# Value sums in four 32-row tiles instead of two 64-row tiles, in a recurrent attention kernel on TensorE

## The chip, the cores and the metric

The kernel runs on one core of one Trainium2 chip. The metric is the device time of one execution in microseconds (us), as the median of several. The engines that matter are TensorE (PE, matmuls; its weight loads are listed as PEld), VectorE (DVE), ScalarE (ACT), GpSimd (POOL) and the DMA queues, of which SyncE (SP) issues most. [...]

## The reference

Two blocks are computed twice, one after the other, on x of 2048 rows by 512. Block A is attention with a recurrent memory: the rows are taken in 64 segments of 32, and each segment sees 8 memory rows ahead of its own 32.

```
for s in range(64):
    h = concat(mem, layernorm(x)[32*s : 32*s + 32])        # 40 rows x 512
    q, k, v = h Wq, h Wk, h Wv                             # 32 heads of 128
    p = softmax(mask(q k^T * scale))                       # 40 x 40 for each head
    o = (p v) Wo                                           # 40 x 512
    mem = o[0:8]                                           # goes into the next segment
    out[s] = o[8:40]
x = x + out
```

The memory rows see everything; of the others, a row sees the memory and the rows up to itself. Block B is a gated MLP with a product over the rows (a 2048 x 2048 matrix). The segments of block A depend on each other through `mem`, so that a segment's projections can't start before the output projection of the one before.

## The kernel before

**Rows of a segment.** Each segment has 8 memory rows and 32 others. The projections of a segment run on 32 rows: the 8 memory rows and the first 24 of the others. The last 8 of each segment's rows are projected ahead, for the four segments of a block of 128 rows together (`b_units`, `b_even`, `b_light`, from line 809), and their output projection follows later (`y_part`). These are the *fill* matmuls: `fill()` issues the next few of them at set places of the segment, a step being mostly 4, 8 or 16 matmuls. Their results (KX, VX and the last columns of QQ) make the "own" part below.

**Heads.** The 32 heads are two halves r of 16. In a half, head 4i + g has index i = 0..3 and group g = 0..3. Group g lies in partitions 32g to 32g + 31: in S and E the partition is 32g + key row.

**One segment** (`segment`, from line 1055) is written out by hand. The order of instructions on PE, DVE and ACT is the order of the code (a manual schedule), so that each engine takes its instructions in this order, and waits between engines are semaphores:

- Projections of q and k, `qk(0)`, `qk(2)`, `qk(1)`, `qk(3)` (L753): ACT copies each to `rows` (L1072), DVE transposes it into QQ or KA (L1075).
- `scores(r)`: 16 matmuls of 40 columns (L1098) and 4 of 64 (L1102) into psS, in column tiles of 32. `exps(r)` (L1107, ACT) writes S.
- `close(r)` (L1110, DVE) multiplies S by a mask and writes E. E is held twice: E[:, r, s] for s = 0, 1 holds the groups with g % 2 = s and zeros for the others, so that one matmul over 64 partitions (two groups) gives both groups' results in columns of their own.
- `v_mm(r)` (L753): the value projections, into psK for half 0 (copied to VA by DVE, L1196) and psV for half 1 (copied to VA by ACT, L1211).
- `sums_zero` (L1121): the softmax sums of half 0's memory rows, 16 matmuls of 64 columns. `inverse` (ACT, L1164 Ln and L1165 Exp) makes 1/sum, Rm.
- `pv(r)`: value sums, 8 matmuls of 80 columns with VA as weights (L1147) and 2 of 128 with VX (L1150), in 64-row tiles into psO[r], two banks for each half.
- `sums_tokens` (L1139) gives the sums of all other rows into psT, `sums_one` (L1130) those of half 1's memory rows into psO[1].
- `memory_out(r)` (L1168, DVE): value sums of the memory rows times Rm, into uT. `spare1` issues spare work between the two.
- The output projection of the memory rows: `wo_pairs` for half 0 (L930, into px) and `wo_rest` for half 1 (L937, into psO[1]'s spare columns); `fold_side`, `fold` and `build_hA` (L1034 to L1047) add the parts and transpose them into hT, where the next segment's projections read them. Fill matmuls stand between.
- Off that path: ACT makes Rt, the inverse of psT (L1245, L1248); DVE writes the token outputs, `tok_out` (L1171) and `last_out` (L1174).

**PSUM** in block A: accA and accB (one bank each, for fills, psm, psV, px), `att` (two banks: psQ, then psS, then psT) and `attO[0]`, `attO[1]` (two banks each; psK uses `attO[0]`, psO[0] and psO[1] both).

The order around the change, of half 1's values and the sums:

```
v_mm(1, psW, (0, 1)); scores(1); exps(1); v_mm(1, psW, (2,)); sums_zero(pN); v_mm(1, psW, (3,))
invert = inverse(0, pN); copy VA[:, 1] (ACT); invert(); close(1)
fill(); pv(0); sums_tokens(psT); sums_one(); pv(1); memory_out(0); spare1(E); fill()
inverse(1, psO[1][:, :, 320:384])(); memory_out(1); wo_pairs(px, uT_cur); wo_rest(pw, uT_cur)
```

Of the kernel before, what the change touches and what calls it, by code (L numbers as in the profile page):

```python
# [14 lines left out]
P = 128  # L15
# [51 lines left out]
def _consts(ctx, tc, c, b_sp, between):  # L67
# [11 lines left out]
    own = maskf[:, 160:224].rearrange("p (i q) -> p i q", i=4)  # L79
# [4 lines left out]
    for q in range(0, P, 32):  # L84
        blk = maskf[q:q + 32, 0:160].rearrange("p (i q) -> p i q", i=4)[:, :, 8:32]
        nc.gpsimd.affine_select(out=blk, in_=blk, compare_op=ALU.is_ge, fill=0.0, base=8,
                                pattern=[[0, 4], [1, 24]], channel_multiplier=-1)
        last = own[q:q + 32, :, 8:16]
        nc.gpsimd.affine_select(out=last, in_=last, compare_op=ALU.is_ge, fill=0.0, base=0,
                                pattern=[[1, 4], [4, 8]], channel_multiplier=-1)  # L90
    maskN = cp.tile([P, 2, 224], BF16, name="maskN")
    nc.vector.memset(maskN[:], 0.0)
    for gs in range(4):
        nc.vector.tensor_copy(maskN[32 * gs:32 * gs + 32, gs % 2, :], maskf[32 * gs:32 * gs + 32, :])
    ones = cp.tile([P, P], BF16, name="ones")
    nc.vector.memset(ones[:], 1.0)
    half = cp.tile([P, 2, 32], BF16, name="half")
    nc.vector.memset(half[:], 0.0)
    for g in range(2):
        nc.vector.memset(half[64 * g:64 * g + 64, g, :], 1.0)  # L100
# [9 lines left out]
    c.update(maskN=maskN, ones=ones, half=half)  # L110
# [596 lines left out]
def a_block(tc, c, rows, front, MV_in, RS_in, MV_out, RS_out, ahead, wo, S, first):  # L707
# [4 lines left out]
    maskN, ones, half = c["maskN"], c["ones"], c["half"]  # L712

    with ExitStack() as ctx:
# [19 lines left out]
        ps_pool = ctx.enter_context(tc.tile_pool(name="a_ps", bufs=1, space=PSUM))  # L734
        ps1_pool = ctx.enter_context(tc.tile_pool(name="a_ps1", bufs=1, space=PSUM))

        accA = _Tagged(acc_pool, "accA", 1)
        accB = _Tagged(acc_pool, "accB", 1)
        att = _Tagged(ps_pool, "att", 1)
        attO = [_Tagged((ps_pool, ps1_pool)[r], f"attO{r}", 1) for r in range(2)]  # L740
# [126 lines left out]
        def early_turn():  # L867

            for k, G in enumerate(EARLY):
                pT = (att, attO[1])[k].tile([P, 2 * DM * 2], BF16, name="pT")  # L870
# [16 lines left out]
        def early_units():  # L887

            for n, (j, G, k) in enumerate((j, G, k) for j, G in ((0, 2), (0, 3), (2, 2)) for k in range(2)):
                ps = (attO[0], attO[1], att)[n % 3].tile([P, 2, 512], F32, name="psP")  # L890
# [164 lines left out]
        def segment(s, fill, spare1, spare2, spare3, tail, loads):  # L1055
# [11 lines left out]
            E = segp.tile([P, 2, 2, 224], BF16, name="E", bufs=1)  # L1067
# [16 lines left out]
            def own(q):  # L1084

                return q.rearrange("p (i b e) -> p i b e", i=4, b=2)
# [4 lines left out]
            def scores(r):  # L1091
# [3 lines left out]
                for i in range(4):  # L1095
                    for g in range(4):
                        n = 4 * i + g
                        mms.append(nc.tensor.matmul(pS[32 * g:32 * g + 32, 40 * i:40 * i + 40], lhsT=KA[:, r, n // 2, :, n % 2], rhs=QQ[:, r, n // 2, :, n % 2],  # L1098
                                                    start=(i == 0), stop=True, tile_position=(0, 32 * g), skip_group_check=True))
                for g in range(4):  # L1100
                    q = QQ[:, r].rearrange("p (i g) q two -> p i g two q", i=4)[:, :, g // 2, g % 2, :]
                    mms.append(nc.tensor.matmul(own(pS[32 * g:32 * g + 32, 160:224]), lhsT=KX[r][:, g, :], rhs=ends(q),  # L1102
# [9 lines left out]
            def e_all(e, lo, hi):  # L1112

                return e[:, :, 0:160].rearrange("p n (i q) -> p n i q", q=40)[:, :, :, lo:hi]

            def e_own(e, b):
                return e[:, :, 160:224].rearrange("p n (i b e) -> p n i b e", i=4, b=2)[:, :, :, b, :]

            def sums_zero(pN):

                return [nc.tensor.matmul(pN[32 * cg:32 * cg + 32, 64 * g:64 * g + 64], lhsT=half[:, g, :], rhs=e_own(E[:, 0], 0) if k else e_all(E[:, 0], 0, 8),  # L1121
                                         start=False, stop=True, tile_position=(0, 32 * cg), skip_group_check=True)
                        for k in range(2) for g in range(2) for cg in range(4)]

            def sums_one():

                for k in range(2):
                    for g in range(2):
                        e = E[64 * g:64 * g + 64, 1]
# [340 lines left out]
```

## Time and profile before

| | |
|---|---|
| median of 3 runs | 1608.67 us (1607.46 to 1610.44) |
| the profiled execution | 1610.67 us, its span 1609.0 us |
| granted TensorE clock | 1.0 |
| instructions | 90845 |
| segments of block A in the span | 128 (64 in each of two passes) |

A row of the timeline gives start and duration in us, engine, line, operation, output<-inputs, the tile (rows*columns of the array, for PE), the shape and a count: instructions of one kind that follow each other closely are one row, with the start of the first and the time that their union covers. The bracket says how long the engine was idle before it and what released it. A row of a group has instead: count, busy us in all, mean ns of one, idle us before them. Matmuls overlap: a matmul's row lasts from the first column going in until the last result, so a row's duration is longer than the step to the next row.

### The profile page before, as it was taken

The numbers are of one execution on the slowest core, as the hardware profiler recorded it, in microseconds if no ns is written. First come the engines' busy times: TensorE is split into PE (matmuls) and PEld (weight loads), VectorE is DVE, ScalarE is ACT, GpSimd is POOL, SyncE is SP. The second block draws the span as 40 slices with busy tenths as digits, with TensorE's granted clock in tenths as the row PEclk, the third lists the DMA queues.
The fourth block names the chain that finished last, engine by engine and source line by source line (L and its number), as shares of the span: only waits on it lengthen the run. The fifth ranks groups of instructions, "written<-read, shape, count | busy, mean of one in ns | idle before, by whom it ended". The sixth has DMA issues, their size and how long they took to land.

```text
span 1609.0 us, 90845 instructions
## 1 busy us (share of the span) xinstructions
PE 1577.9 (98%) x40998; PEld 979.7 (61%) x40998; DVE 1068.8 (66%) x3064; ACT 1052.1 (65%) x2279; POOL 307.5 (19%) x674
## 2 busy tenths in 40 slices
PE   6899999999999999999999999999999999999999
PEld 3566666666666666566656666666666666665565
DVE  3667666667777776784456666666677667768622
ACT  4677777777777777670057777777777777776400
POOL 6211111112211222320011111111222112224000
PEclk9999999999999999999999999999999999999999
DMA  9411221213211332378951112111232123425697
GB/s 360 137 57 43 43 44 45 48 40 76 83 50 40 87 87 61 102 176 176 208 160 45 46 48 46 50 44 50 73 89 72 47 72 95 97 56 174 146 186 169
DMA packets 256861, 149.93 MB, mean 93 GB/s; under 512 B 189592, under 2 KB 232192, under 8 KB 256472
## 3 DMA queue, kind: packets, MB, share of 16 engines
q1 hardware_dynamic: 242552, 97.94, 27.3%
q0 software_dynamic: 13920, 46.18, 8.5%
q8 instruction: 321, 5.26, 1.3%
q14 instruction: 68, 0.56, 0.1%
HBM read 60.21 MB, written 39.55 MB: 62 GB/s over the span
## 4 chain that ended last, share of the span: by engine, by line
PE 56%; DMA 1%; DVE 1%; issue 0%; ACT 0%; SPq 0%; POOL 0%; DVEq 0%; POOLq 0%
PE pg L401 9%; PE psQ L753 7%; PE psK L753 7%; PE psb L753 5%; PE pz L300 4%; PE psO L937 4%; PE px L930 3%; PE psV L753 3%; PE psm L753 3%; PE py L444 3%; PE pwB L949 2%; PE psO L1147 2%; PE psT L1139 1%; PE psS L1098 1%; PE pw L1422 0%; PE psS L1121 0%
## 5 line engine op out<-in xcount | busy, mean ns | idle before, releaser
L753 PEld LDWEIGHTS <-hT 128*32 128x32 bf16 x12288 | 343.5, 96 | 261.4 <-DVE hT L1047 18.3
L753 PE MATMUL psV<-Wv_sb,hT 128*32 128x512 bf16 x2048 | 166.0, 379 | 0.0
L1072 ACT CAST rows<-psQ 128x512 bf16<-128x512 f32 x256 | 144.8, 589 | 24.2 <-PE psQ L753 21.3
L1107 ACT ACTIVATE S<-psS 128x224 bf16<-128x224 f32 x256 | 92.2, 360 | 99.7 <-PE psS L1102 99.5
L1168 DVE TENSOR_TENSOR uT<-psO,Rm 128x128 bf16<-128x128 f32 x256 | 74.7, 292 | 124.2 <-ACT Rm L1165 123.9
L1075 DVE STREAM_TRANSPOSE QQ<-rows 128x256 f32<-128x256 f32 x256 | 112.5, 440 | 66.7 <-ACT rows L1072 63.7
L1075 DVE STREAM_TRANSPOSE KA<-rows 128x256 f32<-128x256 f32 x256 | 113.0, 441 | 63.5 <-ACT rows L1072 60.7
L401 PE MATMUL pg<-z,wspT 128*128 128x344 bf16 x1024 | 154.3, 309 | 0.0
L753 PE MATMUL psK<-Wv_sb,hT 128*32 128x512 bf16 x2048 | 152.2, 378 | 0.0
L1171 DVE TENSOR_TENSOR uT<-psO,Rt 128x384 bf16<-128x384 f32 x256 | 139.9, 547 | 16.7 <-ACT Rt L1248 15.1
L1248 ACT ACTIVATE Rt<-Rt 128x512 f32<-128x512 f32 x256 | 147.3, 622 | 4.1
L937 PE MATMUL psO<-Wo_high,uT 128*32 128x128 bf16 x8192 | 140.6, 219 | 2.4 <-issue 1.6
L753 PE MATMUL psQ<-Wq_sb,hT 128*32 128x512 bf16 x2048 | 135.9, 379 | 2.7 <-DVE hT L219 1.5
L753 PE MATMUL psQ<-Wk_sb,hT 128*32 128x512 bf16 x2048 | 135.2, 379 | 0.0
L753 PE MATMUL psm<-Wq_sb,hT 128*32 128x512 bf16 x2048 | 135.2, 379 | 0.0
L753 PE MATMUL psK<-Wk_sb,hT 128*32 128x512 bf16 x2048 | 135.1, 379 | 0.0
L930 PE MATMUL px<-Wo,uT 128*32 128x256 bf16 x3840 | 133.8, 273 | 0.5 <-issue 0.4
L1245 ACT ACTIVATE Rt<-psT 128x1024 f32<-128x1024 f32 x128 | 131.2, 1025 | 3.1
L401 PEld LDWEIGHTS <-wspT 128*128 128x128 bf16 x1024 | 100.1, 98 | 53.4 <-issue 0.4
L937 PEld LDWEIGHTS <-uT 128*32 128x32 bf16 x8192 | 123.0, 97 | 12.7 <-issue 3.6
L930 PEld LDWEIGHTS <-uT 128*32 128x32 bf16 x4096 | 104.0, 97 | 24.1 <-DVE uT L1168 1.2
L1029 POOL COPY KX<-old 128x128 bf16<-128x128 bf16 x128 | 65.7, 540 | 257.3 <-PE psS L1102 148.9
(221 smaller groups left out, 2886.0 us busy)
## 6 DMA issues: line engine op xcount, KB each, us to landing
o_d<-o_sb SPq DMA_DIRECT2D x126, 64.0 KB
vb_d<-front SPq DMA_DIRECT2D x31, 256.0 KB
VX<-vb_d SPq DMA_DIRECT2D x124, 64.0 KB
ln_x<-xd SPq DMA_DIRECT2D x26, 256.0 KB
y_o<-o_d POOLq DMA_DIRECT2D x22, 256.0 KB, 3.3
xd<-y_o POOLq DMA_DIRECT2D x22, 256.0 KB, 2.8
Wq_sb<-in_A_Wq_dram POOLq DMA_DIRECT2D x8, 512.0 KB, 7.3
Wk_sb<-in_A_Wk_dram POOLq DMA_DIRECT2D x8, 512.0 KB, 9.6
```

The lines of the kernel that those rows point to most:

```text
L401: nc.tensor.matmul(pg[t][:, k, 0:344], lhsT=wsp[t][:, st, :], rhs=z(st, 344 * k, 344 * k + 344), start=(st == 0), stop=(st == NT - 1))
L753: return [nc.tensor.matmul(ps[32 * cg:32 * cg + 32, :], lhsT=lhs(kt, cg), rhs=rhs(kt, cg), start=(kt == 0), stop=(kt == KT - 1), tile_posi ...
L930: nc.tensor.matmul(px[at:at + 32, 0:256], lhsT=lhs[:, h, :], rhs=wo_rhs(h, slice(k + 2, None, -2) if h % 2 else slice(k, None, 2)), start= ...
L937: nc.tensor.matmul(pw[32 * cg:32 * cg + 32, :], lhsT=lhs[:, h, :], rhs=wo_rhs(h, cg), start=False, stop=(h == H - 1), tile_position=(0, 32 ...
L1029: eng.tensor_copy(KX[r][:].rearrange("p g (k i) -> p i g k", i=4), bs["KTB"][:, r].rearrange("p (i g) k -> p i g k", i=4)[:, :, :, 8 * j4: ...
L1072: return r, mms, copy(r[:].rearrange("p (n el two) -> p n el two", n=8, two=2), ps.rearrange("p (n two el) -> p n el two", n=8, two=2))
L1075: nc.vector.transpose(out=(QQ[:, j % 2, :, 0:32] if j < 2 else KA[:, j % 2]).bitcast(F32).rearrange("p n q one -> p n (q one)"), in_=r[:]. ...
L1107: return nc.scalar.activation(out=S[:, r], in_=psS[:, r, 0:224], func=ACT.Exp, scale=scale)
L1168: nc.vector.tensor_tensor(out=hview(uT_cur[:], r, 24, 32), in0=oview(r, 0, 8), in1=Rm[:, r].rearrange("p g (n q) -> p g n q", q=8), op=ALU ...
L1171: nc.vector.tensor_tensor(out=hview(uT_nxt[:], r, 0, 24), in0=oview(r, 8, 32), in1=rview(r, 0, 24), op=ALU.mult)
L1245: nc.scalar.activation(out=Rt[:], in_=psT[:], func=ACT.Ln)
L1248: nc.scalar.activation(out=rt, in_=rt, func=ACT.Exp, scale=-1.0)
```

## The change

- E is held once, [P, 2, 224]: for each i, 40 columns (`0:40`) and 16 columns of the own part (`40:56`). The mask has the same layout, and `scores` writes psS in it.
- `pv(r)` works in tiles of 32 rows: each group g has a matmul of its own (16 of 40 columns and 4 of 64) into a PSUM bank of its own; both halves share these four banks (columns 160r and up). `sums_one` does the same with 8 matmuls of 32 columns.
- `sums_zero` takes 8 matmuls of 32 columns and stands directly behind `scores(1)`. `divide` (DVE, a reciprocal and a product) divides half 0's memory columns of E ahead of `pv(0)`, so that `memory_out(0)` is a copy. `inverse` is gone; Rm is made for half 1 alone.
- VA's half 0 is copied by ACT and no longer by DVE.
- `sums_tokens` stands behind `pv(1)` and has 8 matmuls (256 and 64 columns) in 64-row tiles, with weights `pick` that are one for one of the two groups.
- `attO` is one tile of four banks; psK uses its first two. Three pools `pre` take the place of `att` and `attO` for the work ahead of the first segment, and are closed before it.

```
-                nc.vector.tensor_tensor(out=E[:, r], in0=S[:, r].unsqueeze(1).to_broadcast([P, 2, 224]), in1=maskN[:], op=ALU.mult)
+                nc.vector.tensor_tensor(out=E[:, r], in0=S[:, r], in1=mask[:], op=ALU.mult)
...
+                return [nc.tensor.matmul(pN[32 * g:32 * g + 32, :], lhsT=group[:, g, :], rhs=E4[:, 0, :, 40 * k:40 * k + 8],
+                                         start=False, stop=True, tile_position=(0, 32 * g), skip_group_check=True)
+                        for k in range(2) for g in range(4)]
+            def divide(pN):
+                rc = segp.tile([P, 32], F32, name="rc", bufs=1)
+                read = nc.vector.reciprocal(out=rc[:], in_=pN)
+                e = E[:, 0].rearrange("p (i c e) -> p i c e", i=4, e=8)[:, :, 0:6:5, :]
+                nc.vector.tensor_tensor(out=e, in0=e, in1=rc[:].rearrange("p (i e) -> p i e", i=4).unsqueeze(2).to_broadcast([P, 4, 2, 8]), op=ALU.mult)
+                return read
+            def tile32(out, g, lhsT, rhs, start):
+                return nc.tensor.matmul(out, lhsT=lhsT, rhs=rhs, start=start, stop=True, tile_position=(32 * g, 0), skip_group_check=True)
...
+                    for n in range(2):
+                        for g in range(2):
+                            e = E4[64 * g:64 * g + 64].rearrange("p r i c -> p (r i) c")
+                            o = psT[:, g, 256 * n:256 * n + 256].rearrange("p (n q) -> p n q", q=32)
+                            nc.tensor.matmul(o[:, :, 24:32] if k else o, lhsT=pick[64 * g:64 * g + 64, n, :], rhs=e[:, :, 48:56] if k else e[:, :, 8:40],
+                                             start=(k == 0 and n == 0), stop=True, skip_group_check=True)
...
                 for i in range(4):
-                    for g in range(2):
-                        o = psO[r][:, g, 0:320].rearrange("p (s i q) -> p s i q", s=2, i=4)[:, :, i, :]
-                        nc.tensor.matmul(o, lhsT=VA[64 * g:64 * g + 64, r, i, :], rhs=E[64 * g:64 * g + 64, r, :, 40 * i:40 * i + 40],
-                                         start=(r == 0 and i == 0), stop=True, skip_group_check=True)
+                    for g in range(4):
+                        at = 160 * r + 40 * i
+                        tile32(psO[:, g, at:at + 40], g, of(VA, g)[:, r, i, :], of(E4, g)[:, r, i, 0:40], r == 0 and i == 0)
...
+                if r == 0:
+                    nc.vector.tensor_copy(hview(uT_cur[:], 0, 24, 32), oview(0, 0, 8))
...
-            nc.vector.tensor_copy(VA[:, 0].rearrange("p i e -> p (i e)"), psK[:, 1, :])
+            nc.scalar.copy(VA[:, 0].rearrange("p i e -> p (i e)"), psK[:, 1, :])
...
-            v_mm(1, psW, (2,))
-            pN = psS[:, 0, 224:352]
+            pN = psS[:, 0, 224:256]
             other_bank(sums_zero(pN), expd)
-            v_mm(1, psW, (3,))
-            Rm = segp.tile([P, 2, 2, 64], F32, name="Rm", bufs=1)
-            invert = inverse(0, pN.rearrange("p (g q) -> p g q", g=2))
+            other_bank([divide(pN)], expd)
+            v_mm(1, psW, (2, 3))
             nc.scalar.copy(VA[:, 1].rearrange("p i e -> p (i e)"), psW[:])
-            invert()
             close(1)
-            psO = [attO[r].tile([P, 2, 512], F32, name="psO") for r in range(2)]
+            psO = attO.tile([P, 4, 512], F32, name="psO")
...
             pv(0)
             psT = att.tile([P, 2, 512], F32, name="psT")
-            sums_tokens(psT)
             sums_one()
             pv(1)
+            sums_tokens()
             memory_out(0)
...
-            inverse(1, psO[1][:, :, 320:384])()
+            Rm = segp.tile([P, 4, 32], F32, name="Rm", bufs=1)
+            nc.scalar.activation(out=Rm[:], in_=psO[:, :, 320:352], func=ACT.Ln)
+            nc.scalar.activation(out=Rm[:], in_=Rm[:], func=ACT.Exp, scale=-1.0)
             memory_out(1)
```

More of the change, by code (lines that the diff above doesn't have):

```diff
@@ L109, in _consts @@
     tctx.close()
-    c.update(maskN=maskN, ones=ones, half=half)
+    c.update(mask=mask, ones=ones, group=group, pick=pick)
     return c
@@ L711, in a_block @@
     scale = float(DH) ** -0.5
-    maskN, ones, half = c["maskN"], c["ones"], c["half"]
+    mask, ones, group, pick = c["mask"], c["ones"], c["group"], c["pick"]
     with ExitStack() as ctx:
@@ L1125, in sums_one, with of @@
+            def tile32(out, g, lhsT, rhs, start):
+                return nc.tensor.matmul(out, lhsT=lhsT, rhs=rhs, start=start, stop=True, tile_position=(32 * g, 0), skip_group_check=True)
+            def of(t, g):
+                return t[32 * g:32 * g + 32]
             def sums_one():
                 for k in range(2):
[L1128 to L1131 removed]
```

96 lines of the change are left out of this document (43 added, 53 removed).

## Prediction, on record before the changed kernel ran

> **What bounds the kernel now.** I read the page first, then the timeline of one recurrent segment out of the middle (400 to 410 us), then the groups by form for means over all segments. From the page:
>
> ```profile
> PE 1577.9 (98%) x40998; PEld 979.7 (61%) x40998; DVE 1068.8 (66%) x3064; ACT 1052.1 (65%) x2279; POOL 307.5 (19%) x674
> PEclk9999999999999999999999999999999999999999
> ```
>
> TensorE is 98% busy at full clock. A busy share does not show short gaps, because a matmul's row runs on after its columns have gone in; so I go by the starts in the timeline (start, duration, engine, line, out<-in, count).
>
> ```profile
> 400.44 1.05 PE L753 MATMUL psQ<-Wq_sb,hT 128*32 128x512 bf16 x16
> ...
> 401.93 0.28 DVE L1174 TENSOR_TENSOR front<-psO,Rt 128x128 bf16<-128x128 f32 x1
> ...
> 403.04 1.05 PE L753 MATMUL psK<-Wk_sb,hT 128*32 128x512 bf16 x16
> ...
> 404.13 0.28 PE L1098 MATMUL psS<-QQ,KA 128*32 128x40 bf16 x16
> ...
> 404.24 0.20 PE L1102 MATMUL psS<-QQ,KX 128*32 128x64 bf16 x4
> ...
> 404.27 0.82 PE L753 MATMUL psK<-Wv_sb,hT 128*32 128x512 bf16 x12
> ...
> 405.39 0.68 DVE L1196 CAST VA<-psK 128x512 bf16<-128x512 f32 x1
> ...
> 405.45 0.20 PE L1102 MATMUL psS<-QQ,KX 128*32 128x64 bf16 x4
> ...
> 405.48 0.39 PE L753 MATMUL psV<-Wv_sb,hT 128*32 128x512 bf16 x4
> ...
> 405.70 0.29 PE L1121 MATMUL psS<-E,half 128*32 128x64 bf16 x16
> 405.74 0.36 ACT L1107 ACTIVATE S<-psS 128x224 bf16<-128x224 f32 x1 [0.76 <-PE psS L1102]
> ...
> 405.81 0.39 PE L753 MATMUL psV<-Wv_sb,hT 128*32 128x512 bf16 x4
> ...
> 406.03 0.39 PE L949 MATMUL pwB<-Wo,old 128*32 128x512 bf16 x4
> ...
> 406.25 0.59 ACT L1211 CAST VA<-psV 128x512 bf16<-128x512 f32 x1
> ...
> 406.35 0.32 PE L1147 MATMUL psO<-E,VA 64*128 64x80 bf16 x8
> ...
> 406.50 0.22 PE L1150 MATMUL psO<-E,VX 64*128 64x128 bf16 x2
> ...
> 406.58 0.45 PE L1139 MATMUL psT<-E,ones 64*128 64x512 bf16 x4
> ...
> 406.86 0.22 PE L1130 MATMUL psO<-E,ones 64*128 64x64 bf16 x4
> ...
> 406.92 0.31 PE L1147 MATMUL psO<-E,VA 64*128 64x80 bf16 x8
> ...
> 407.06 0.22 PE L1150 MATMUL psO<-E,VX 64*128 64x128 bf16 x2
> 407.08 0.29 DVE L1168 TENSOR_TENSOR uT<-psO,Rm 128x128 bf16<-128x128 f32 x1 [0.56 <-ACT Rm L1165]
> ...
> 407.21 0.40 PE L949 MATMUL pwB<-Wo,old 128*32 128x512 bf16 x4
> ...
> 407.32 0.28 ACT L1164 ACTIVATE Rm<-psO 128x128 f32<-128x128 f32 x1 [0.28 <-PE psO L1150]
> ...
> 407.44 1.04 PE L930 MATMUL px<-Wo,uT 128*32 128x256 bf16 x30
> 407.63 0.31 ACT L1165 ACTIVATE Rm<-Rm 128x128 f32<-128x128 f32 x1
> 407.98 0.29 DVE L1168 TENSOR_TENSOR uT<-psO,Rm 128x128 bf16<-128x128 f32 x1 [0.27 <-ACT Rm L1165]
> 408.21 0.28 PE L930 MATMUL px<-Wo_high,uT 128*32 128x256 bf16 x2
> ...
> 408.32 1.08 PE L937 MATMUL psO<-Wo_high,uT 128*32 128x128 bf16 x64
> ...
> 410.15 1.05 PE L753 MATMUL psQ<-Wq_sb,hT 128*32 128x512 bf16 x16
> ```
>
> Four facts are to be seen. (1) Next to nothing on PE waits: each row starts when the columns of the row before are in (four matmuls of 512 columns side by side: 405.81 to 406.03, 0.22 us). (2) Where the tile shape changes, about 0.10 is added: 406.03 to 406.35 is 0.32 for the same 0.22 of columns, and 407.06 to 407.21 is 0.15 for two matmuls of 128 columns side by side (0.055). (3) Narrow matmuls have a floor: sixteen of 40 columns take 404.13 to 404.24, 0.028 per four, where columns alone would take 0.017. (4) A second chain runs level with PE. VA's half 1 is copied by ACT until 406.84, and `pv(1)` uses it at 406.92: the token sums (L1139, 0.28) and L1130 (0.06) are what PE does meanwhile. After the last matmul of `pv(1)` (407.06) come Ln at 407.32, Exp, and the division L1168, which ends at 408.27; L937, which needs it, starts at 408.32. So a hand-over between engines costs 0.04 to 0.05.
>
> **The change part by part.** I take the order and the waits of the built program, and put the durations above on them. The scores of half 1 end at 405.48 in both.
>
> *Memory sums (`sums_zero`).* 16 matmuls of 64 columns (405.70 to 405.81, 0.11) become 8 of 32: two groups of four at the floor, 0.055. They move ahead of two value projections, which then run as eight (0.43): these end at 405.97, the last four having started at 405.75 and not 405.81.
>
> *`divide`, new on DVE.* It waits for these sums (last group at 405.51, 0.20 for such a row as L1102's, 0.05 to hand over: 405.76), and `pv(0)` waits for it. Two rows give DVE's price per column:
>
> ```profile
> L1196 DVE CAST VA<-psK 128x512 bf16<-128x512 f32 x128 | 87.1, 680 | 0.1
> ...
> L1038 DVE COPY cross<-px 64x128 f32<-64x128 f32 x128 | 36.3, 284 | 42.5 <-PE px L930 41.8
> ```
>
> 384 columns cost 396 ns more, 1.03 ns each over 0.15 fixed; so by estimate 0.19 for the reciprocal of 32 columns and 0.22 for the product of 64: done at 406.22 with the hand-over. PE is ready at 406.29 (fill of four and the shape change, 0.32, after 405.97): covered by 0.07. The trace has no reciprocal. Its floor is 0.15, which gains nothing; as upper end I take the dearest DVE row here, 0.68. Then the product, `close(1)` behind it and `sums_one` come so late that `pv(1)` starts near 407.1, another 0.3 a segment. I take 0.19, since these rows are linear in columns; even 0.4 stays hidden behind the wait below.
>
> *Value sums in 32-row tiles.* `pv` goes from 8 matmuls of 80 and 2 of 128 to 16 of 40 and 4 of 64. Four 32-row tiles side by side do not occur in the trace. From below: floor of fact 3, five groups at 0.028, 0.14. From above: only pairs of weight loads go side by side (as with 64 rows), 0.056 a group, 0.28. I take 0.14, as the four column tiles of L1098 are the nearest row. `sums_one` stays at 0.06 (two groups against two pairs). So `pv(0)` runs 406.29 to 406.43 and `sums_one` to 406.49.
>
> *The wait that takes their place.* `pv(1)` still needs VA's half 1. Its copy starts when the last four projections, begun at 405.75, are through: 0.06 earlier than before, at 406.19; 0.59 later it ends at 406.78, and `pv(1)` starts at **406.83**. PE has nothing to do from 406.49 on, because the token sums are now issued behind `pv(1)` and PE takes matmuls in order: a wait of 0.34, only 0.09 earlier than today. Queued behind it on PE are the token sums, the fill and both output projections.
>
> *Token sums last.* The same columns (two pairs of 256 for one of 512): 0.27. But they are 64-row tiles behind 32-row ones. [...] I take 0.095. PE then: `pv(1)` to 406.97, change, 407.07, sums to 407.34, change, 407.43. Today the fill starts at 407.21: **+0.22**. With fill 0.23, px 0.77 and its last pair 0.11, L937 is reached at 408.54.
>
> *Half 0's output and the chain.* `memory_out(0)` no longer waits for Rm, but half 0 and half 1 now lie in the same four banks, and the built program makes it wait for the last matmul of `pv(1)` and makes the Ln of half 1 wait for it. Today these overlap: DVE reads half 0 at 407.08 to 407.37 while ACT reads half 1 from 407.32. [...] Chain: last matmul of `pv(1)` 406.955, +0.26 to DVE at 407.215, copy 0.284 (L1038's), hand-over 0.04, Ln at 407.54; from Ln to L937 1.00 as today: 408.54. Again **+0.22**. DVE holds its spare work and ACT its copies behind these waits; both have gaps there.
>
> *The rest is off the path.* VA's half 0 moves from DVE (0.68) to ACT: its matmuls end at 405.09 (404.27 + 0.82), so it runs 405.14 to 405.73, and the exponentials of half 1 start at 405.74 today. Behind those, 0.34 of slack would hide a delay. Two activations of 0.28 and 0.31 go from ACT; `close` writes half as much. `psK` now shares its banks with both halves, so it waits for the last token output of half 1: 402.21 against 403.04 here, and in a fuller segment
>
> ```profile
> 411.97 0.28 DVE L1174 TENSOR_TENSOR front<-psO,Rt 128x128 bf16<-128x128 f32 x1
> ...
> 412.75 1.04 PE L753 MATMUL psK<-Wk_sb,hT 128*32 128x512 bf16 x16
> ```
>
> 0.50 is left: no cost unless DVE falls back by that. A few more constant fills at the start, at most 1 us once. No DMA is touched.
>
> *Sum.* Half of the segments (b_units and the last block's y_part: 64 of 128) have eight fill matmuls before px, and room in the chain:
>
> ```profile
> 1048.98 0.29 DVE L1168 TENSOR_TENSOR uT<-psO,Rm 128x128 bf16<-128x128 f32 x1 [0.60 <-ACT Rm L1165]
> ...
> 1049.43 0.28 PE L930 MATMUL px<-Wo_high,uT 128*32 128x256 bf16 x2
> 1049.54 1.07 PE L937 MATMUL psO<-Wo_high,uT 128*32 128x128 bf16 x64
> ```
>
> Here L1168 ends 0.27 before L937, so PE's +0.22 counts alone; in the other 64 both do. The copy of half 1 and its 128 segments:
>
> ```profile
> L1211 ACT CAST VA<-psV 128x512 bf16<-128x512 f32 x128 | 75.0, 586 | 0.0
> ```
>
> 128 x 0.22 = +28.2 us. The profiled execution took 1610.67 (span 1609.0 and 1.67 around it), so 1638.8; the median of the runs is 2.0 below it: **1637**.
>
> **The rivals.**
> *No drain between 32 and 64 rows.* PE's shift is 0.125, the chain's stays 0.22: 64 x 0.125 + 64 x 0.22 = 22 us, 1631. For it: the columns are 128 wide in both. Against: both changes seen cost 0.10.
> *Four-row groups at half rate.* 0.056 a group: `pv(0)` hides in the wait, `pv(1)` takes 0.14 more on both paths, 0.36 a segment, 1655. For it: the trace never shows four row tiles. Against: L1098's four column tiles.
> *A slow reciprocal.* 0.68 as above: 0.3 more, up to 1675; against it, the linear rows.
> *Faster: the matmul stream decides.* If `pv(1)` followed `sums_one` at 406.49, the stretch from 405.48 to the fill would be 0.055 + 0.43 + 0.32 + 0.14 + 0.06 + 0.14 + 0.095 + 0.27 + 0.095 = 1.60 against 1.73 today: 128 x -0.13 = -17 us, 1592. It decides if VA's half 1 is in place by 406.44, when the row has it end 0.59 after a start at 406.19. [...] Only a much shorter copy would save it.
>
> **How the numbers follow.** Forecast 1637, 57%; no drain 1631, 17%; half rate 1655, 11%; slow reciprocal 4%; faster 1592, 7%; smaller terms of mine all on one side, so that it ends between: 4%, half of it within 0.2%. 0.2% is about what a measurement of this kernel can tell from no change. The range reaches from below the second case, with a copy of half 0 shorter than 0.284, to the third: 1622 to 1657. Faster 0.07, same 0.02, slower 0.91.
>
> **What would show it.** In the changed kernel: PE idle or a stretched step of some 0.34 before `pv(1)`, ended by ACT's VA; the first matmul of `pv(1)` 0.05 behind the end of that copy; `memory_out(0)`, Ln, Exp, `memory_out(1)` strictly one after the other; 0.10 before the token sums; the segment, here 9.71 from one psQ to the next (400.44 to 410.15), grown by 0.22. It is wrong if `pv(1)` follows `sums_one` at once, or if the segment grows less than 0.1.

## The result, and the profile after

The changed kernel takes **1695.01 us** (median of 4 runs, 1691.84 to 1695.7) against 1609.56 for the kernel before (4 runs, 1607.46 to 1613.36): ratio 1.0521, interval 1.0506 to 1.0537. The profiled execution took 1695.12, its span grew from 1609.0 to 1693.4: +84.4 us, where 28 were forecast.

From the page of the kernel after, then one row of the page of the kernel before (DMA queues: packets, MB, share of 16 engines):

```profile
span 1693.4 us, 95510 instructions
...
PE 1588.8 (94%) x43526; PEld 996.4 (59%) x43558; DVE 1027.7 (61%) x3195; ACT 1089.2 (64%) x2151; POOL 293.8 (17%) x674
...
PEclk9999999999999999999999999999999999999999
...
q8 instruction: 341, 5.59, 1.4%
```

```profile
q8 instruction: 321, 5.26, 1.3%
```

The granted clock is as before (1.0 then, 0.999 now). PE's busy time grew by only 11 us (1577.9 to 1588.8), though its share fell from 98% to 94%: the rest is idle. The waits of PE (waiting line, what ended the wait: us in total, times, longest), first of the kernel after, then of the kernel before:

```profile
PE psO L935 <- issue: 38.5, 51, 1.2
PE psO L1126 <- DVE E L1122: 35.4, 128, 1.8
```

```profile
PE psO L937 <- issue: 1.6, 5, 0.4
```

In the kernel after, the weight loads of L935 wait longer than its matmuls, because a matmul's row still runs when the gap begins; their row gives the gaps whole, 47.7 us:

```profile
PEld L935 <- issue: 47.7, 52, 1.4
```

Two waits are new. One stands before L1126, which is `tile32`, the value sums; it comes 128 times, once a segment, and the forecast had it one step later. The other was in no forecast: 51 long gaps ahead of matmuls of L935 (the output projection, L937 before), which wait for **nothing that the profile shows** ("issue"). Both are in this segment of the timeline of the kernel after:

```profile
408.62 0.21 PE L1101 MATMUL psS<-QQ,KX 128*32 128x64 bf16 x4
...
408.65 0.23 PE L1113 MATMUL psS<-E,group 128*32 128x32 bf16 x8
...
409.01 0.36 DVE L1120 RECIPROCAL rc<-psS 128x32 f32<-128x32 f32 x1 [0.47 <-PE psS L1113]
409.13 0.42 PE L947 MATMUL pwB<-Wo,old 128*32 128x512 bf16 x4
409.38 0.59 ACT L1211 CAST VA<-psV 128x512 bf16<-128x512 f32 x1
409.40 0.23 DVE L1122 TENSOR_TENSOR E<-E,rc 128x64 bf16<-128x64 bf16 x1
...
409.77 0.28 PE L1126 MATMUL psO<-E,VA 32*128 32x40 bf16 x16 [0.21 <-DVE E L1122]
...
409.88 0.21 PE L1126 MATMUL psO<-E,VX 32*128 32x64 bf16 x4
...
410.02 0.27 PE L1126 MATMUL psO<-E,VA 32*128 32x40 bf16 x16
...
410.13 0.19 PE L1126 MATMUL psO<-E,VX 32*128 32x64 bf16 x4
...
410.26 0.45 PE L1144 MATMUL psT<-E,pick 64*128 64x256 bf16 x8
410.40 0.29 DVE L1168 CAST uT<-psO 128x128 bf16<-128x128 f32 x1 [0.59 <-PE psO L1126]
...
410.73 0.28 ACT L1227 ACTIVATE Rm<-psO 128x128 f32<-128x128 f32 x1 [0.76 <-DVE uT L1168]
...
410.87 1.04 PE L928 MATMUL px<-Wo,uT 128*32 128x256 bf16 x30
411.04 0.31 ACT L1228 ACTIVATE Rm<-Rm 128x128 f32<-128x128 f32 x1
411.38 0.29 DVE L1170 TENSOR_TENSOR uT<-psO,Rm 128x128 bf16<-128x128 f32 x1 [0.35 <-ACT Rm L1228]
...
411.74 1.00 PE L935 MATMUL psO<-Wo_high,uT 128*32 128x128 bf16 x57
...
413.35 0.29 PE L935 MATMUL psO<-Wo_high,uT 128*32 128x128 bf16 x7 [0.61 <-issue]
```

The upper part is the forecast's chain, rank for rank. The last two rows are the surprise: after 57 of its 64 matmuls L935 stops, and the other seven start 0.6 us later, though their operands have lain ready since 411.67, when L1170 ended. The next segments show that it is not the work itself: the first has no gap, the second has one after 54 matmuls.

```profile
422.48 1.08 PE L935 MATMUL psO<-Wo_high,uT 128*32 128x128 bf16 x64
...
432.55 0.95 PE L935 MATMUL psO<-Wo_high,uT 128*32 128x128 bf16 x54
...
434.34 0.34 PE L935 MATMUL psO<-Wo_high,uT 128*32 128x128 bf16 x10 [0.84 <-issue]
```

**What the gaps have in common.** Counted over PE's records (each matmul is a weight load, PEld, and a matmul), they fall on one index modulo 256: 184 in the first half of the program, 173 in the second. In the traces of the other runs it is 193, in both halves wherever gaps are many; the trace of the kernel after lacks 32 of its matmul records (43526 against 43558 weight loads), which moves the count. The page's queue row fits: PE's 43526 + 43558 records and its 284 semaphore waits and drains, divided by 341 transfers, are 256, and 5.59 MB over 341 are 16.4 KB each; before, 2 x 40998 and 217 over 321 are again 256. So the instruction queue made one transfer of 16.4 KB for every 256 of PE's instructions, and the gaps stand where one such **block of 256 instructions** ends. A segment with four fill matmuls ahead of px has 602 records before and 642 after, one with eight has 618 and 658 (20 matmuls more, two records each): about two and a half blocks, which is why the boundary falls into L935 in every second segment.

Over all block boundaries outside the first and last segments of each half of the program (counted from the index on which the gaps add up to most; ns; a block's use is the time from its first to its last instruction):

```
use of the block     before: n, mean gap, use+gap     after: n, mean gap, use+gap
under 3000                  7     78   3036              41    945   3559
3000 to 3400               52    103   3368              44    240   3501
3400 to 4200              108     48   3789             101    104   3773
over 4200                 121     22   4980             121      9   5020
```

After the change, a block that PE gets through in under 3.4 us is followed by a gap, such that use and gap make about 3.5 us on average; a longer one hardly is. Before, the dense stretch from `pv(0)` to L937 hardly ever got through 256 in under 3.0 us; after, 41 blocks do.

**What ends a gap.** By these counts there is one transfer for each block. In the 14 traces of this case, 605 of the block boundaries inside block A have a gap above 0.3 us, and 574 of these gaps end 1.2 to 1.6 us after the landing of the transfer that came last (median 1.41). Of all 4279 boundaries, with and without a gap, 12 came sooner than 1.2 us after it. So the end of a gap goes with a landing, which I read as the arrival of the next block. The transfers themselves did not become slower: 1.07 us on average before, 1.08 after. What differs for the dense blocks is their start: in the first row of the table, the transfer began 0.43 us after the block's first instruction before and 1.04 after, which is why the seven dense blocks of the kernel before have hardly a gap. 1.04, 1.08 and 1.4 add up to the 3.5 us.

One dense block behind a slow one is enough for a gap: 42 of the 62 gaps above 0.3 us in the kernel after stand behind a block whose predecessor took over 4.2 us.

**Where the 84.4 us are.** For the 59 segments with four fill matmuls ahead of px and 62 with eight (the rest are first, last or mixed ones), I take the medians of four steps (to the last scores matmul, to the first of L935/L937, through that row without gaps, to the next segment); their sum is the segment without stalls, and what the lengths have above it is stall.

```
                         before            after
segment without stalls   9.674 / 10.032    9.980 / 10.328 us
stalls, 121 segments     12.3              56.2 us
```

The chain: 59 x 0.306 + 62 x 0.296 = 36 us. The stalls: 44 us. The remaining segments, together: 4 us.

### The profile page after: what moved, and what is told of

Read it like the earlier page. It is cut to its first block, busy times and chain, and to the rows that moved or that the text cites. A ratio compares the mean times of both kernels' runs of the same rounds, so it can differ in the third digit from the quotient of the medians.

```text
span 1693.4 us, 95510 instructions
## 1 busy us (share of the span) xinstructions
PE 1588.8 (94%) x43526; PEld 996.4 (59%) x43558; DVE 1027.7 (61%) x3195; ACT 1089.2 (64%) x2151; POOL 293.8 (17%) x674
## 3 DMA queue, kind: packets, MB, share of 16 engines
q8 instruction: 341, 5.59, 1.4%
## 4 chain that ended last, share of the span: by engine, by line
PE 50%; DVE 4%; issue 2%; DMA 1%; POOL 0%; ACT 0%; SPq 0%; DVEq 0%
PE pg L404 9%; PE psQ L751 6%; PE psK L751 6%; PE psb L751 4%; PE psO L935 4%; PE px L928 3%; PE psm L751 3%; PE pz L303 3%; PE py L447 2%; PE psO L1126 2%; PE psV L751 2%; PE psT L1144 1%; DVE rc L1120 1%; PE pwB L947 1%; DVE E L1122 1%
## 5 line engine op out<-in xcount | busy, mean ns | idle before, releaser
L751 PEld LDWEIGHTS <-hT 128*32 128x32 bf16 x12288 | 338.8, 96 | 262.9 <-DVE hT L1045 20.9
L935 PE MATMUL psO<-Wo_high,uT 128*32 128x128 bf16 x8192 | 149.0, 219 | 38.6 <-issue 38.5
L751 PE MATMUL psV<-Wv_sb,hT 128*32 128x512 bf16 x2048 | 159.9, 380 | 0.0
L935 PEld LDWEIGHTS <-uT 128*32 128x32 bf16 x8192 | 124.9, 97 | 55.7 <-issue 47.7
L751 PE MATMUL psK<-Wv_sb,hT 128*32 128x512 bf16 x2048 | 153.1, 378 | 0.0
L751 PE MATMUL psQ<-Wq_sb,hT 128*32 128x512 bf16 x2048 | 136.1, 379 | 3.3 <-DVE hT L222 1.8
L751 PE MATMUL psK<-Wk_sb,hT 128*32 128x512 bf16 x2048 | 136.1, 379 | 0.3 <-issue 0.3
L751 PE MATMUL psQ<-Wk_sb,hT 128*32 128x512 bf16 x2048 | 135.8, 379 | 0.0
L751 PE MATMUL psm<-Wq_sb,hT 128*32 128x512 bf16 x2048 | 135.7, 379 | 0.0
L928 PEld LDWEIGHTS <-uT 128*32 128x32 bf16 x4096 | 107.9, 97 | 22.0 <-issue 2.5
L1027 POOL COPY KX<-old 128x128 bf16<-128x128 bf16 x128 | 58.6, 485 | 287.7 <-PE psS L1101 179.3
L1027 POOL COPY KX<-front 128x128 bf16<-128x128 bf16 x126 | 57.0, 483 | 286.1 <-PE psS L1101 170.8
L1227 ACT ACTIVATE Rm<-psO 128x128 f32<-128x128 f32 x128 | 35.6, 278 | 110.0 <-DVE uT L1168 110.0
```

Of the source, the lines that this page charges most:

```text
L751: return [nc.tensor.matmul(ps[32 * cg:32 * cg + 32, :], lhsT=lhs(kt, cg), rhs=rhs(kt, cg), start=(kt == 0), stop=(kt == KT - 1), tile_posi ...
L928: nc.tensor.matmul(px[at:at + 32, 0:256], lhsT=lhs[:, h, :], rhs=wo_rhs(h, slice(k + 2, None, -2) if h % 2 else slice(k, None, 2)), start= ...
L935: nc.tensor.matmul(pw[32 * cg:32 * cg + 32, :], lhsT=lhs[:, h, :], rhs=wo_rhs(h, cg), start=False, stop=(h == H - 1), tile_position=(0, 32 ...
L1027: eng.tensor_copy(KX[r][:].rearrange("p g (k i) -> p i g k", i=4), bs["KTB"][:, r].rearrange("p (i g) k -> p i g k", i=4)[:, :, :, 8 * j4: ...
L1227: nc.scalar.activation(out=Rm[:], in_=psO[:, :, 320:352], func=ACT.Ln)
```

## The experiments

Theory: two separate costs, the chain that was forecast (a little dearer), and the arrival of PE's instructions. Rivals: the gaps belong to the 32-row tiles or to the new order; or they are only the other face of the waits and go with them. Each expectation was on record before its run. All results first; "without stalls" and "stalls" as above, "gaps" are those above 0.15 us at the block boundaries; "records" are PE's in a segment with four fills (a mean); each ratio is against the kernel before on the same chip (1615.95 for a1 to a4, 1616.25 for a5 to b3, 1615.62 for c1 to c4). That is 6 to 7 us more than in the first two rows, so runs of different rows are best compared by their ratios.

```
                    us       ratio, interval           records  without stalls   stalls  gaps
before (profile)    1609.56  1                         602       9.674 / 10.032   12.3    7.2
after (profile)     1695.01  1.0521  1.0506 to 1.0537  642       9.980 / 10.328   56.2   51.1
a1_shift            1700.19  1.0529  1.0496 to 1.0563  642       9.995 / 10.334   54.2   48.3
a2_nodivide         1669.83  1.0340  1.0315 to 1.0366  641       9.941 / 10.295   37.4   31.2
a3_half0            1704.77  1.0539  1.0494 to 1.0584  642       9.971 / 10.379   60.6   60.0
a4_neither          1661.09  1.0278  1.0245 to 1.0310  641       9.640 / 10.022   65.1   56.5
a5_rows64           1689.41  1.0452  1.0430 to 1.0475  611      10.170 / 10.489   28.5   19.6
b1_tokens_last      1636.32  1.0125  1.0110 to 1.0140  602       9.927 / 10.287    7.1    7.3
b2_dense            1673.68  1.0363  1.0342 to 1.0383  642       9.897 / 10.263   45.4   39.1
b3_spread           1658.74  1.0265  1.0245 to 1.0284  642       9.842 / 10.200   37.1   27.3
c1_after_pairs24    1706.95  1.0570  1.0551 to 1.0589  610      10.419 / 10.618   16.8   24.0
c2_before_pairs20   1624.08  1.0053  1.0039 to 1.0067  586       9.911 / 10.105   11.1    9.0
c3_before_pairs24   1650.03  1.0211  1.0195 to 1.0226  570      10.129 / 10.324    4.8    6.3
c4_rows64_all       1675.69  1.0371  1.0351 to 1.0391  611       9.998 / 10.362   30.9   23.4
```

**a1_shift.** The kernel after, with the transposes of `early_turn` (once, ahead of all segments) issued five times: all later instructions move against the block boundaries.

```diff
-                for kt in range(KT):
+                for kt in 5 * tuple(range(KT)):
                     nc.tensor.transpose(pT[:, P * kt:P * kt + P], rows.early[G]...
```

> The changed kernel with 32 transposes more ahead of the first segment (each of eight is done five times; the result is the same): 64 PE instructions once, under 2 us of work. Instruction theory (the gaps inside L935 come where a block of 256 PE instructions ends and the next has not arrived): the gaps keep their segments, every second one, but stand 64 instructions earlier in the program, after about 25 of the 64 matmuls and not after 57, and are shorter, near 0.5 us, since more of the slow instructions ahead fall into the block: 30 to 38 us in all for 47. Time 8 to 14 us below the changed kernel. Bank theory (the gaps come from what DVE and ACT do with the four shared PSUM banks): they stay after 57 matmuls, 47 us in all, and the time rises by the 1 to 2 us of work.

From a1's waits of PE:

```profile
PE psO L935 <- issue: 23.0, 34, 1.5
PE psb L751 <- issue: 7.1, 11, 1.4
```

The gaps move. In each of the 20 segments that have one above 0.3 us inside L935 in both traces, it stands 31 or 32 matmuls earlier than in the kernel after, which is the 64 instructions that were added (a matmul is two); so the gaps belong to a place in the program's count, not to L935's work. The weight loads of L935 wait 30.4 us, within the 30 to 38 expected. The time was missed: 8 to 14 us less were expected, and the ratio is that of the kernel after (1.0529 and 1.0521), because in other segments the boundary now falls into L751, the row behind, whose weight loads wait 28.8 us on "issue" and not 13.9.

**a2_nodivide, a3_half0, a4_neither.** The two waits, taken away one at a time and together. a2 leaves out the division of half 0's columns (its output is scaled by a constant instead); a3 lets `pv(1)` use the values of half 0, which are long there, in place of half 1's; a4 does both.

```diff
 a2, a4
-            other_bank([divide(pN)], expd)
-                    nc.vector.tensor_copy(hview(uT_cur[:], 0, 24, 32), oview(0, 0, 8))
+                    nc.vector.tensor_scalar(out=hview(uT_cur[:], 0, 24, 32), in0=oview(0, 0, 8), scalar1=1.0 / 40, scalar2=None, op0=ALU.mult)
 a3, a4
-                        tile32(psO[:, g, at:at + 40], g, of(VA, g)[:, r, i, :], ...
+                        tile32(psO[:, g, at:at + 40], g, of(VA, g)[:, 0, i, :], ...
```

> The changed kernel without the reciprocal and the product of divide; half 0's memory sums are scaled by 1/40 in place of the division (outputs differ). Theory: pv(0) no longer waits, but pv(1) still waits for ACT's copy of VA's half 1, 1.38 us after the scores of half 1, so that the time stays within 6 us of the changed kernel. Rival, that DVE's divide is what costs (44 us of idle PE stand before pv(0)): 30 to 40 us faster.

> The changed kernel with pv(1) taking VA's half 0 as its weights, so that it does not wait for ACT's copy of half 1, which is still made (outputs differ). Theory: pv(0) still waits for divide until 1.13 us after the scores, and pv(1) follows 0.19 later, at 1.33 and not 1.38: 4 to 9 us faster. Rival, that the copy alone sets the pace: 30 us faster or more.

> Both together: no divide (half 0 scaled by 1/40) and pv(1) with VA's half 0 (outputs differ). Theory of two waits that cover each other: now pv(0) starts near 0.81 and pv(1) near 1.0 us after the scores, 0.3 to 0.38 earlier, and the time falls by 36 to 46 us against the changed kernel, far more than the other two together. The gaps inside L935 stay or grow (45 to 60 us), as the same instructions are taken in less time; so the kernel is still slower than before, at 1640 to 1658 us. If the gaps were tied to the waits, they would vanish and the time would be near 1600.

The starts after the last scores matmul (medians, us; the first class of segments):

```
              pv(0)    pv(1)    px       L935/L937
before        0.886    1.455    1.974    2.859
after         1.135    1.383    2.266    3.158
a2_nodivide   0.849    1.380
a3_half0               1.380
a4_neither    0.848    1.047             2.803
```

Without the division `pv(1)` starts at 1.380, held by VA; without VA's wait it starts at 1.380, held by the division; without both at 1.047. **Two waits that end at the same moment hide each other**: for the start of `pv(1)`, one alone is worth nothing, both are worth 0.33. The median of 1.135 in the kernel after lies in one of two groups: in some segments `pv(0)` starts at 1.13 and `pv(1)` 0.25 later, when VA has come; in the others `pv(0)` starts at 1.21 and `pv(1)` follows directly, 0.185 later. The first waits of a2, then of a3:

```profile
PE psO L1126 <- ACT VA L1210: 19.2, 116, 0.4
PE psO L935 <- issue: 10.9, 17, 1.8
```

```profile
PE psO L935 <- issue: 43.9, 50, 1.9
PE psO L1126 <- DVE E L1122: 33.9, 127, 1.8
```

Yet a2's expectation, within 6 us of the kernel after, was missed: its profiled span is 25 us below (1668.4), near the 30 to 40 of its rival, though not for the rival's reason. Only 4 of the 25 are in the segment without stalls; 19 are stalls. In a2 PE's pause stands between `pv(0)` and `pv(1)`, inside the dense stretch, where it gives the next block time to arrive; in the kernel after and in a3 it stands ahead of the stretch. That fits, but no run moved the pause alone. a4 is the clearest: without stalls its segment is shorter than that of the kernel *before* (9.640 against 9.674), and it is still 2.8% slower, with the most stalls of all. a4's drop against the kernel after is the one expected (by the ratios 39 us, for 36 to 46), though its 1661.09 is 3 us above the range on record; a3, expected 4 to 9 us faster than the kernel after, is no faster (1.0539 and 1.0521). The first of a4's waits:

```profile
PE psO L935 <- issue: 24.2, 35, 1.5
PE psb L751 <- issue: 6.6, 18, 0.7
```

**a5_rows64, c4_rows64_all.** The value sums of the kernel after in 64-row tiles, which takes 16 matmuls out of each segment; c4 has `sums_one` in 64-row tiles too. Both leave out that each group's values and sums are its own.

```diff
 a5 and c4, pv (VX alike)
-                for i in range(4):
-                    for g in range(4):
-                        at = 160 * r + 40 * i
-                        tile32(psO[:, g, at:at + 40], g, of(VA, g)[:, r, i, :], ...
+                for i in range(2):
+                    for b in range(4):
+                        g, at = b % 2, 160 * r + 80 * i
+                        nc.tensor.matmul(psO[:, b, at:at + 80], lhsT=VA[64 * g:64 * g + 64, r, i, :], ...
 c4, sums_one
-                    for g in range(4):
-                        tile32(psO[:, g, 320:352], g, of(ones, g), ...
+                    for b in range(4):
+                        g = b % 2
+                        nc.tensor.matmul(psO[:, b, 320:352], lhsT=ones[64 * g:64 * g + 64, :], ...
```

> The changed kernel with pv back in 64-row tiles: for each half 8 matmuls of 80 columns and 4 of 64, for 16 of 40 and 4 of 64, into the same four banks; two groups are summed together, so half 0 is scaled by 1/2 and half 1's sums count double (outputs differ). 16 matmuls, 32 PE instructions fewer in a segment, and no change of tile shape ahead of the token sums. Instruction theory: the gaps inside L935 fall from 47 us to under 15; with 12 us less for the shape change and 5 to 10 more for wider pv, the time is 1645 to 1662 us. Bank theory: gaps stay near 47, time 1685 to 1695.

> The 64-row version of the kernel after with sums_one in 64-row tiles too (which leaves out that each group's sums are its own): the matmuls of the value sums, of sums_one and of the token sums all lie in 64-row tiles, the count of matmuls is that of the 64-row version before it. Theory: the two changes of mode around sums_one go, so that pv(1) stands where VA's copy lets it and the last output matmul 0.3 earlier than in that version (3.398/3.522 down to about 3.08/3.28); stalls some 30 to 45 us, since the blocks pass more quickly than there; 1689 falls to 1650 to 1670. Rival (the 64-row version was held by something other than the changes of mode): 1680 or more.

With 611 records in a segment the stalls halve (56 to 29 and 31). From a5's waits of PE, and from its page, where the queue brings 16 blocks fewer than in the kernel after:

```profile
PE psO L935 <- issue: 10.0, 18, 1.3
```

```profile
q8 instruction: 325, 5.32, 1.4%
```

a5's time was missed by 27 us: I had overlooked that `sums_one`, left in 32-row tiles between two stretches of 64-row ones, adds two changes of tile shape. c4 takes them away and gains 0.17 and 0.13 a segment (and 14 us), about half of the 0.3 expected; `pv(1)` starts at 1.49, not at 1.38. From `pv(0)` to `pv(1)`, where neither waits, a5 takes 0.46, c4 0.30 and the kernel after 0.185: the 64-row tiles are the slower ones here, and they stand behind the division. c4's 1675.69 is 6 us above the range on record.

**b1_tokens_last.** The kernel before, with one edit: the token sums behind `pv(1)`.

```diff
-            sums_tokens(psT)
             sums_one()
             pv(1)
+            sums_tokens(psT)
```

> The kernel before with one thing changed: the token sums are issued behind pv(1), as in the changed kernel. Theory of the lost cover: pv(1) starts at best 0.03 earlier, because it waits for ACT's copy of VA's half 1, and the token sums' 0.28 us come on top: 0.25 a segment, 1637 to 1645 us. Rival, that the order of the sums does not matter: within 3 us of before.

`pv(1)` starts 0.03 earlier, px 0.26 later, and the segment without stalls grows by 0.25: this order alone costs most of the chain's 0.30. The median grew by 20 us, where the sum of the segments without stalls gives 31 for these 121; 5 of the difference are stalls that went (12.3 to 7.1), and the rest is that the kernel before is slower on this chip: the profiled spans grew by 25.4 (1609.0 to 1634.4).

**b2_dense, b3_spread.** The kernel before, with 20 matmuls of four columns added in each segment into unused columns: as many as the change adds. In b2 they stand in the dense stretch behind `pv(0)`, in b3 behind the scores of half 0.

```diff
 b2
             pv(0)
+            for n in range(20):
+                g = n % 2
+                nc.tensor.matmul(psO[0][:, g, 508:512], lhsT=ones[64 * g:64 * g + 64, :], ...
 b3
             scores(0)
+            for n in range(20):
+                g = n % 4
+                nc.tensor.matmul(psS[32 * g:32 * g + 32, 0, 508:512], lhsT=KA[:, 0, n // 4, :, 0], ...
```

> The kernel before with 20 matmuls of 4 columns more behind pv(0) of each segment, into unused columns of its bank (the result is the same), so that the segment has as many PE instructions as in the changed kernel, in the same stretch. Their own time: ten pairs at the 0.028 floor, 0.28 a segment, 36 us. Instruction theory: gaps of 0.3 to 0.9 us appear inside L937 or beside it in about half of the segments, 25 to 50 us in all, and the time is 1670 to 1695 us. Bank theory: no gaps beyond today's 4 us, 1643 to 1650.

> The kernel before with the same 20 matmuls of 4 columns, but behind the scores of half 0, between value projections of 512 columns, where PE takes few instructions per us. Their own time: five groups of four at 0.028, 0.14 a segment, 18 us. Instruction theory in the form that the density decides: gaps as before, under 10 us, 1624 to 1634 us. If the count per segment alone decided, the gaps would be those of the run with the 20 behind pv(0).

The first wait of b2 at L937, then that of b3:

```profile
PE psO L937 <- issue: 18.1, 37, 1.1
```

```profile
PE psO L937 <- issue: 5.3, 13, 0.8
```

Nothing of the change is in b2 but its number of instructions, and the stalls come: 12 to 45 us. That decides against the rivals. b3 missed its expectation of under 10: 37 us. Its blocks are seldom under 3.0 us (10 against 44 in b2), but 64 lie between 3.0 and 3.4; so the number in a whole segment counts too, not only the density of its end.

**c1_after_pairs24, c2_before_pairs20, c3_before_pairs24.** More heads of the output projection in px, where a head takes two matmuls of 256 columns, not four of 128: the same columns, 16, 8 and 16 matmuls fewer.

```diff
-WO_PAIR = 16
+WO_PAIR = 24
```

> The kernel after, with WO_PAIR 24 instead of 16: eight more heads go through px with two matmuls of 256 columns instead of four of 128. The same columns, 16 matmuls fewer in each segment (all of them behind pv), nothing else changed. Theory (instruction arrival: blocks of 256 PE instructions, each some 3.5 us after the one before at the earliest): the gaps within L935 fall from 47 us to under 25, all stalls from 57 us to some 30 as in the 64-row version, which had 16 fewer too; 1696 falls to 1665 to 1675. The heads 16 to 23 need the output of half 1, so px waits at head 16, where L935 waited before; the fold of px begins 0.44 later, which may cost up to 0.1 in a segment (13 us). Rival (the gaps come from the 32-row tiles themselves, or from the order of the sums, not from the number of instructions): no change, 1690 to 1702, gaps of L935 still over 40 us.

> The kernel before with WO_PAIR 20: 8 matmuls fewer in each segment, the same columns. Theory (instruction arrival): before has some 12 us of stalls, of which 3 to 6 go; the fold begins 0.22 later and should be covered by the rest of the heads: 0.2 to 0.4% faster than before. Rival (before has no stall to lose, since none of its gaps is in L937): same within 0.1%.

> The kernel before with WO_PAIR 24: 16 matmuls fewer in each segment. Theory (instruction arrival): 5 to 9 us of the 12 us of stalls go, 0.3 to 0.6% faster, if the fold of px, which begins 0.44 later, stays off the path; if it does not, DVE's fold ends up to 0.1 later in a segment, which is 13 us, and the kernel is slower by up to 0.4% with fewer stalls. Rival (no stall to lose): no gain, or only the loss.

The stalls did what the theory says: in c1 56 to 17 us, the gaps within L935 from 47 to 17; in c3 12 to 5. But all three are slower than the kernels that they were made from, and their times were missed (c1 1706.95 us for 1665 to 1675; c2 0.5% slower than before and c3 2.1%, where c2 was expected 0.2 to 0.4% faster and c3 at worst 0.4% slower), by a wait that I had overlooked. c3's wait, and its place in the timeline:

```profile
PE psb L753 <- DVE t L1040: 21.2, 61, 0.7
```

```profile
402.01 0.62 PE L937 MATMUL psO<-Wo_high,uT 128*32 128x128 bf16 x32
...
402.63 0.29 DVE L1040 TENSOR_TENSOR t<-px,cross 128x128 f32<-128x128 f32 x1
...
402.97 1.05 PE L753 MATMUL psb<-Wq_sb,hB 128*32 128x512 bf16 x16 [0.34 <-DVE t L1040]
```

psb takes over px's buffer (both are `accB`'s, which has one), so it waits until the fold has read px; with px longer and L937 shorter nothing is left to cover the fold. It costs 0.46 and 0.29 a segment in c3, 0.24 and 0.07 in c2, more than the stalls that go. None of the versions beats the kernel before.

## Why the prediction was wrong

The sign and the chain were right; the size was not. **The failed step is the sum, "128 x 0.22 = +28.2 us": it has no term for the arrival of instructions.** Its ground was fact (1), "Next to nothing on PE waits", true of the kernel before and carried over to one with 20 matmuls more in a segment, which I had counted for their columns and floors only. Term: 44 us (56.2 of stalls against 12.3). The chain was mis-sized besides, 36 us for 28, but with it alone the time would have been near 1646, inside the range on record. The page of the kernel before held a warning that I passed over: 321 transfers of 16.4 KB in its instruction queue, and 59 of its 288 blocks already used in under 3.4 us.

Step by step:

- *The wait that takes the place of VA's* (forecast: `pv(1)` at 406.83, which is 1.35 after the last scores): measured 1.383. VA's copy ended at 409.97 and `pv(1)` began at 410.02, the forecast 0.05. The start is right in cause and size; the idle time of PE that was to stand before it stands mostly ahead of `pv(0)` (next point).
- *`divide`* (0.19 for the reciprocal, "covered by 0.07"): wrong by itself, without effect on the end. In the groups by form:

```profile
L1120 DVE RECIPROCAL rc<-psS 128x32 f32<-128x32 f32 x128 | 45.7, 357 | 60.4 <-PE psS L1113 60.4
...
L1122 DVE TENSOR_TENSOR E<-E,rc 128x64 bf16<-128x64 bf16 x128 | 34.4, 269 | 4.4
```

  357 ns, not 190: the copies' price per column did not hold for this reciprocal. The product took 269, not 220, and the hand-overs from PE to DVE and back 0.13 and 0.14, not 0.05. So most of PE's idle time stands before `pv(0)`, at 1.135, and not before `pv(1)`. That "even 0.4 stays hidden behind the wait below" held, to within 0.01 (a2, a3), and that is luck: the reciprocal, the product and the hand-overs together took 0.39 more than forecast, where 0.07 and the wait of 0.34 were there to cover it. The rival of the slow reciprocal, which starts at 0.68, did not come about.
- *0.14 for each half of the value sums*: 409.77 to 409.88 is 0.11 for four groups of 40 columns, the floor of 0.028 each. The rival of half rate is refuted.
- *The change between 32-row and 64-row tiles* (0.095): my estimate, from two changes of other shapes that added 0.10 and 0.095 before; the trace before has none between 32 and 64 rows. In the kernel after, 410.13 to 410.26 is 0.13 for four matmuls whose floor is 0.028, so 0.10. The rival in which this change costs nothing is refuted.
- *`memory_out(0)` in the chain*: the group of L1227 shows it 128 times:

```profile
L1227 ACT ACTIVATE Rm<-psO 128x128 f32<-128x128 f32 x128 | 35.6, 278 | 110.0 <-DVE uT L1168 110.0
```

  and DVE, Ln, Exp, DVE stand one after another at 410.40, 410.73, 411.04 and 411.38, as forecast.
- *+0.22 in a segment*: 0.30. `pv(1)` was 0.03 later than forecast and the stretch from there to px 0.05 longer (0.88 for 0.83).
- *The faster rival* ("the matmul stream decides", -0.13 a segment, 1592): a4 made its condition true. The segment without stalls became 0.03 and 0.01 shorter, and the kernel was still 2.8% slower. With these stalls the rival would not have come true even so.

The cause is settled as far as this: a number of instructions, added without anything else, brings the stalls (b2); fewer instructions take them away (a5, c1, c3); shifting the program moves them (a1); and 574 of the 605 gaps above 0.3 us end 1.2 to 1.6 us after the landing of a transfer of the instruction queue. In the segment shown above the boundary was crossed at about 409.90, the queue's next transfer began at 411.15 and took 0.96, and PE went on at 413.35, 1.24 after the landing. Open is what decides when a transfer begins, and what fills the time from its landing to PE's next instruction.

## What to carry to other kernels

Before splitting matmuls into smaller tiles, count PE's instructions, weight loads included, in the densest stretch, and compare its time per 256 (the block of this case) with the gaps that the trace already has; a split that is free in columns and floors may be paid for in instructions, as here, where 20 matmuls more in a segment brought 44 us of stalls. When two waits end at the same moment, taking away one does not show what it costs: take away both before judging either. And a stretch that holds an engine may cover something else that is late: moving the token sums uncovered VA's copy, and shortening L937 uncovered the fold of px.

## What the runs showed of the hardware

- The instruction queue made one transfer of 16.4 KB for every 256 of PE's instructions (341 transfers in the kernel after, 321 before). In the kernel after, such a block used in under 3.4 us was followed by a gap that made use and gap 3.5 us on average; in L935 the gaps were up to 1.4 us, and "issue" is what the waits name as their end.
- A transfer took 1.07 us on average before and 1.08 after. All but 12 of 4279 blocks began 1.2 us or more after the last transfer had landed, and the gaps ended 1.41 us after it (median).
- A RECIPROCAL of 128x32 from PSUM took 357 ns on DVE, where a copy of 64x128 took 284.
- Four 32-row tiles side by side ran at the floor of the column tiles, 0.028 us a group; the change from 32-row to 64-row tiles took 0.10.
